# First stage of a fused attention and two-expert kernel: the first chunk's scores ahead of its decays, the gate tables on two queues

## The chip, the cores and the metric

The kernel runs on one core of a Trainium2 chip. The metric is the device time of one execution in microseconds (us), lower is better. [...] The other engines are VectorE (DVE), ScalarE (ACT), GpSimd (POOL) and SyncE (SP), which here only issues DMAs.

## The reference, cut to what matters

```python
for t in range(S):                                  # B, H, S, D = 4, 8, 768, 40
    m_new = maximum(f_gate[t] + m, i_gate[t])       # running maximum of the gates
    f_stab = exp(f_gate[t] + m - m_new); i_stab = exp(i_gate[t] - m_new); m = m_new
    C = f_stab * C + i_stab * outer(v[t], k[t])     # state of each head, 40 x 40
    n = f_stab * n + i_stab * k[t]
    y[t] = sigmoid(o_gate[t]) * (C @ q[t]) / maximum(abs(n @ q[t]), 1)
x = moe(y)      # 3072 tokens of 320: each goes to one of 8 experts, 320 -> 1024 -> 320, times its gates
return moe2(x)  # (sigmoid(x @ w_gate) * (x @ w_val)) @ w_out, 320 -> 1536 -> 320
```

## The kernel before, in words

The recurrence over 768 positions is computed in chunks of T = 128, six to a sequence, 24 in all (`NTILE`). Within a chunk the output is (scores times decays) times values, with the decay of two positions as the exponential of a difference of running gate sums; between chunks a state of 40 x 41 per head is carried. The gates are worked out for all 32 rows (sequence and head) at once, in two halves of 384 positions: `gates(x)` (L477) is a chain on VectorE of a scan, five elementwise operations and a second scan, with two roundings on ScalarE (L493, L496) and a subtraction on GpSimd (L485). `store(x)` (L508) writes four results to two DRAM tables, `L_d` and `a_d`; `decay(u)` (L412) reads them back, spread over partitions, into the operands `at` and `rt` for three chunks at a time. `pattern_at` and `pattern_rt` (L468, L473) fill the fixed rows of these operands. `factors(x)` and `exps(x)` (L516, L522) make the per-token factors; `to_end(x)` (L527) transposes them on TensorE into `tm` and makes the gate totals `gt` by one more product, from `own_g`.

For a chunk, `dec` (L636) makes the exponents of the decays in PSUM (for chunk 0 directly from the gates, with small products, L642 to L647; for the others from `at` and `rt`, L651), `exp` (L653) the decays, `sc` (L657) the scores of q and k, `pf` (L662) their product, each in two groups g of four heads. `out_` (L675) multiplies by the values, `inter` (L685) adds the carried state, `kw` (L670, GpSimd) and `state` (L700) make the chunk's own state, `Cm`, `C`, `cb` carry it on. `den`, `th` (tanh of the output gate, ScalarE, L739), `th1` (adds 1, GpSimd, L742), `sod` (GpSimd) and `x` finish the attention; `xh`, `xla`, `xl`, `tr`, `log` make the split row and its routing logits; `route` ranks tokens, and `scatter` (L848, GpSimd) writes each 128 rows to their experts' places in DRAM. The first expert's job reads the first 16 tiles of rows back with a transposing DMA (L337).

Every engine runs its instructions in the order in which the program issues them, and every DMA is issued from one engine's queue in that order. `begin()` (L547) and `first()` (L588) issue the stage up to the end of chunk 0. After that `step(n)` (L927) walks the list `ORDER` (L40), where `name:lag` issues that part for chunk n - lag, and `r:k` takes up to k pieces from the generator `step.route`. In step 1 that generator is `rest` (L620): the remaining pieces of the second half's gates, its store, factors, pattern, exponentials, `decay(1)` and chunk 3's loads, in this order. `step` issues the loads of chunk n + 2 at its start, on SP, for n > 1 (L936), so those of chunk 4 stand ahead of `decay(1)` and of chunk 3's. `warm(n)` (L613) issues products of zeros whose results nobody reads; `WARM` = 22 of them open the program.

After the attention come the experts' jobs and the second block (L1112 on), where three quarters of the time lie and nothing changes.

## Time and profile before

| what | us |
|---|---|
| median of 3 runs | 727.23 |
| lowest, highest | 726.78, 731.73 |
| the profiled execution | 726.39 |
| its span | 724.3 |
| TensorE busy in the span | 698.8 |

The span reaches from the first to the last instruction that the profile records; the execution's time is 2.1 us longer. Starts in the timelines count from the span's start. A stretch is read from the windows, which give each engine's busy time in it and the granted clock; a wait is read from the timeline, whose bracket behind an instruction gives the idle time of its engine ahead of it and what ended that.

### The profile page before, as it was taken

To read this page: it belongs to the slowest core of one execution; us is meant where nothing else is said; L and a number is where in the kernel's file an instruction comes from. 1 tells how busy PE (TensorE), PEld (TensorE's weight loads), DVE (VectorE), ACT (ScalarE), POOL (GpSimd) and SP (SyncE) were. 2 spreads that over 40 slices of the span, in tenths; PEclk is the share of its full clock that TensorE was granted. 3 is DMA by queue.
4 is the path that set the end of the run, shared out by engine and by line. 5 is a ranking of instruction groups with operands and counts; after the bars stand their busy time and mean duration, and the time that the engine had idled before them with its cause. 6 is when DMAs were issued, how large, how long until landed. Compare 5 with 4: busy or idle time off the path is not lost. (4 is left out here: it accounts for less than half of the span.)

```text
span 724.3 us, 15451 instructions
## 1 busy us (share of the span) xinstructions
PE 698.8 (96%) x6048; PEld 495.2 (68%) x6048; DVE 396.7 (55%) x912; ACT 328.1 (45%) x782; POOL 144.8 (20%) x172
## 2 busy tenths in 40 slices
PE   8899999869999999999989999999999999999998
PEld 5799998857666775667656676666666666666665
DVE  6767678627788879898877810322403223032230
ACT  5477787625575666654545511322313223132231
POOL 5456788842211121221100000000000000000000
PEclk8799999988999999999999999999999999999999
DMA  6466667543999998873525013001020020000000
GB/s 192 130 183 178 199 185 215 174 143 87 273 297 292 266 274 234 253 232 108 139 59 138 21 35 76 0 19 37 1 55 1 10 47 1 28 1 10 19 0 28
DMA packets 67131, 84.02 MB, mean 116 GB/s; under 512 B 41401, under 2 KB 48970, under 8 KB 67058
## 3 DMA queue, kind: packets, MB, share of 16 engines
q1 hardware_dynamic: 63824, 73.35, 36.1%
q0 software_dynamic: 2640, 9.33, 3.6%
q8 instruction: 48, 0.79, 0.5%
q10 hardware_dynamic: 594, 0.35, 0.2%
q14 instruction: 25, 0.20, 0.1%
HBM read 57.53 MB, written 17.16 MB: 103 GB/s over the span
## 5 line engine op out<-in xcount | busy, mean ns | idle before, releaser
L125 PE MATMUL pa<-xT,wgv 128*128 128x384 f16 x1536 | 250.9, 326 | 2.8 <-DVE hh L1166 2.1
L125 PEld LDWEIGHTS <-wgv 128*128 128x128 f16 x1536 | 150.2, 98 | 102.2 <-issue 3.4
L1161 DVE SCALAR_TENSOR_TENSOR gt<-pa,sg 128x384 f32<-128x384 f32 x96 | 53.5, 557 | 224.2 <-PE pa L125 193.3
L1179 PE MATMUL pb<-wo,hh 128*128 128x320 f16 x864 | 118.5, 299 | 0.0
L1160 ACT ACTIVATE sg<-pa 128x384 f32<-128x384 f32 x96 | 47.0, 490 | 143.7 <-PE pa L125 143.7
L1179 PEld LDWEIGHTS <-hh 128*128 128x128 f16 x864 | 84.5, 98 | 33.2
L358 PE MATMUL pb<-w,hh 128*128 128x320 f16 (+4 forms) x624 | 86.6, 299 | 0.0
L125 PE MATMUL pa<-xT,w 128*128 128x384 f16 (+5 forms) x576 | 80.9, 301 | 1.6 <-DVE hh L348 1.6
L358 PEld LDWEIGHTS <-hh 128*128 128x128 f16 (+4 forms) x624 | 62.8, 101 | 22.3 <-DVE hh L348 0.5
L125 PEld LDWEIGHTS <-w 128*128 128x128 f16 x640 | 55.7, 98 | 32.6 <-issue 2.6
L112 DVE SCALAR_TENSOR_TENSOR w<-ws,w 128x512 f16<-128x512 f32 (+1 forms) x92 | 56.1, 642 | 4.7 <-ACT w L111 3.9
L111 ACT ACTIVATE w<-ws 128x512 f16<-128x512 f32 (+1 forms) x92 | 50.3, 592 | 13.1 <-DMA ws<-in_w 11.7
L1181 ACT ACTIVATE ob<-pb 128x320 f32<-128x320 f32 x24 | 10.5, 437 | 100.5 <-PE pb L1179 100.5
L660 PE MATMUL ps<-qk 128*128 128x128 f32 x384 | 53.9, 287 | 0.0
L1166 DVE TENSOR_TENSOR hh<-gt,hh 128x384 f16<-128x384 f32 x96 | 52.7, 549 | 0.7
L369 POOL DMA_INDIRECT y_d<-yr,own x24 | 28.0, 1167 | 125.0 <-ACT w L111 19.5
L1165 ACT ACTIVATE hh<-gt 128x384 f16<-128x384 f32 x96 | 49.4, 515 | 5.9 <-DVE gt L1161 5.9
L660 PEld LDWEIGHTS ps<-qk 128*128 128x128 f32 x384 | 49.9, 203 | 1.0 <-issue 0.2
L665 DVE TENSOR_TENSOR pf<-ps,w 128x512 f32<-128x512 f32 x48 | 33.0, 686 | 21.7 <-ACT w L655 11.4
L347 ACT ACTIVATE hh<-pa 128x384 f16<-128x384 f32 (+6 forms) x80 | 33.4, 431 | 13.8 <-PE pa L125 13.1
L348 DVE SCALAR_TENSOR_TENSOR hh<-pa,hh 128x384 f16<-128x384 f32 (+6 forms) x80 | 36.3, 480 | 3.9 <-ACT hh L347 3.6
L655 ACT ACTIVATE w<-pw 128x512 f32<-128x512 f32 x48 | 28.3, 592 | 1.4 <-PE pw L651 0.5
(185 smaller groups left out, 716.5 us busy)
## 6 DMA issues: line engine op xcount, KB each, us to landing
ws<-in_w SPq DMA_DIRECT2D x24, 512.0 KB
vk<-in_vk SPq DMA_DIRECT2D x24, 324.0 KB
qk<-in_qk SPq DMA_DIRECT2D x48, 160.0 KB
ws<-in_w SPq DMA_DIRECT2D x15, 480.0 KB
ws<-in_wg SPq DMA_DIRECT2D x9, 512.0 KB
ws<-in_wv SPq DMA_DIRECT2D x9, 512.0 KB
ws<-in_wo SPq DMA_DIRECT2D x8, 480.0 KB
out<-ob SPq DMA_DIRECT2D x24, 160.0 KB
```

The source lines that it names most:

```text
L111: A.activation(hi, src, AF.Copy, scale=scale)
L112: low = lambda: V.scalar_tensor_tensor(lo, src, scale, hi, ALU.mult, ALU.subtract)
L125: PE.matmul(ps, r if swap else l, l if swap else r, start=n == 0, stop=n == len(steps) - 1)
L347: A.activation(self.hh[:, 0, f], ph, AF.Relu)
L348: V.scalar_tensor_tensor(self.hh[:, 1, f], ph, 0.0, self.hh[:, 0, f], ALU.max, ALU.subtract)
L358: PE.matmul(py, self.hh[:, x, k, sl], w2[:, y, k, :], start=k == 0 and x + y == 0, stop=k == K1 - 1 and x == 1)
L660: PE.matmul(m.ps[g][:, p, :], m.k2[:, g, p], m.q2[:, p], start=True, stop=True)
L1160: A.activation(sg, pgv[0], AF.Sigmoid, scale=1.0 / (SY * SWG))
L1161: V.scalar_tensor_tensor(gt, pgv[1], SGT / (SY * SWV), sg, ALU.mult, ALU.mult)
L1165: A.activation(self.gh[:, 0, f, :], box[0], AF.Copy)
L1166: V.tensor_sub(self.gh[:, 1, f, :], box[0], self.gh[:, 0, f, :])
L1179: PE.matmul(po, self.gh[:, x, k, sl], wo[:, y, k * DM:(k + 1) * DM], start=k == 0 and x + y == 0, stop=k == K2 - 1 and x == 1)
```

## The change

The scores of chunk 0 are issued ahead of its decays, those of chunk 1 at the end of the first stage (`sc0`, `sc1` leave step 1). `store` and the reads of `a_d` take a queue; for the first half it is ScalarE's, while `L_d` stays on SP. Chunk 1's loads move ahead of the first half's store, `c32` ahead of chunk 0's values, chunk 2's loads behind the zeroing of their buffer, which moves from GpSimd to ScalarE. Output gates and constants are issued by GpSimd, later than before. Factors and pattern of the first half change places; the second half's pattern is copied by ScalarE. The second half's gates begin in step 1 and not in `first()`. `to_end` hands back its last product as `spread`, which is issued later. Three warm-up products at the end of `first()` go, two come at the start. `th1` moves from GpSimd to VectorE.

```diff
         def decay(u):
+            rows(u, SP_)
+            blocks(u)
+
+        def rows(u, queue):
+            c0 = u % 2 * HC
+            tk = slice(c0 * T, (c0 + HC) * T)
+            src = a_d[:, :, u // 2 * 2:u // 2 * 2 + 2, tk].rearrange("n h g s -> (n h) g s")
+            for i in range(2):
+                queue.dma_start(out=at[0:8, i, :, tk], in_=src)
+
+        def blocks(u):
             b, c0 = u // 2, u % 2 * HC
             c1 = c0 + HC
-            tk = slice(c0 * T, c1 * T)
-            src = a_d[:, :, 2 * b:2 * b + 2, tk].rearrange("n h g s -> (n h) g s")
-            for i in range(2):
-                SP_.dma_start(out=at[0:8, i, :, tk], in_=src)
             for g in range(2):
...
                 copy(at[:, k].rearrange("p g (c t) -> p g c t", t=T)[:, :, cs],
                      cat[:, k:k + 1, :].unsqueeze(1).to_broadcast([KM, 2, len(range(NC)[cs]), T]))
-        def pattern_rt(cs):
-            V.tensor_copy(rt[:, :, cs].rearrange("p g c h t -> p g c (h t)"),
-                          crt.rearrange("p h t -> p (h t)").unsqueeze(1).unsqueeze(1).to_broadcast([KM, 2, len(range(NC)[cs]), NP * T]))
+        def pattern_rt(cs, copy):
+            copy(rt[:, :, cs].rearrange("p g c h t -> p g c (h t)"),
+                 crt.rearrange("p h t -> p (h t)").unsqueeze(1).unsqueeze(1).to_broadcast([KM, 2, len(range(NC)[cs]), NP * T]))
         def gates(x):
...
             SP_.dma_start(out=L_d.rearrange("n g x -> (n g x)").rearrange("(p x y) -> p x y", p=128, y=n),
                           in_=zr.unsqueeze(1).to_broadcast([128, 2, n]))
-        def store(x):
+        def store(x, queue):
             h = half(x)
...
                 SP_.dma_start(out=blocks, in_=c3(aL[:, 2 + n, h]))
-                SP_.dma_start(out=a_d[n].rearrange("h g s -> g h s")[:, :, h], in_=aL[:, n, h])
+                queue.dma_start(out=a_d[n].rearrange("h g s -> g h s")[:, :, h], in_=aL[:, n, h])
         def factors(x, eng):
...
                             c3(fg[:, half(x)])[:, :, T - 1].unsqueeze(1).to_broadcast([R, B * NP, HC]), ALU.mult)
-            pl = psC.tile([128, B * NP * HC], F32, name="pl", tag="c")
-            PE.matmul(pl, side, own.rearrange("r b c -> r (b c)"), start=True, stop=True)
-            V.tensor_copy(gt[:, x].rearrange("q b p c -> q (b p c)"), pl)
+
+            def spread():
+                pl = psC.tile([128, B * NP * HC], F32, name="pl", tag="c")
+                PE.matmul(pl, side, own.rearrange("r b c -> r (b c)"), start=True, stop=True)
+                V.tensor_copy(gt[:, x].rearrange("q b p c -> q (b p c)"), pl)
+
+            return spread
         blank = small.tile([1, 8], F32, name="blank", bufs=1)
         DIRECT = 1
...
             load_qk(chunks[0])
+            SP_.dma_start(out=c32, in_=a["c32"])
             load_v(chunks[0])
-            SP_.dma_start(out=c32, in_=a["c32"])
             zeros = kws[1].rearrange("p h x -> p (h x)")
             copy(qks[1].rearrange("q x p t -> q x (p t)"), zeros.unsqueeze(1).to_broadcast([128, 3, NP * T]))
+            load_qk(chunks[1])
+            load_v(chunks[1])
             pattern_at(H0, copy)
...
                 pass
-
-            G.tensor_copy(blank, L[0:1, S // 2 - 8:S // 2])
-            output_gates(0, G)
-            G.memset(qks[2], 0.0)
-            output_gates(1, G)
-            pattern_rt(H0)
+            store(0, A)
             factors(0, V)
-            store(0)
-            load_qk(chunks[1])
-            load_v(chunks[1])
-            decay(0)
             exps(0)
+            pattern_rt(H0, V.tensor_copy)
+            blocks(0)
+
+        def first():
+
+            m = chunks[0]
+            copy = lambda o, i: A.activation(o, i, AF.Copy)
+            zeros = kws[1].rearrange("p h x -> p (h x)")
+            for g in range(2):
+                sc(m, g)
+            warm(2)
+            for g in range(2):
+                dec(m, g)
+            for g in range(2):
+                exp(m, g)
+                pf(m, g)
+            spread = to_end(0)
+            rows(0, A)
+            copy(qks[2].rearrange("q x p t -> q x (p t)"), zeros.unsqueeze(1).to_broadcast([128, 3, NP * T]))
+            for t in Cbs:
+                copy(t.rearrange("q p j d -> q (p j d)"), zeros[:, :NP * 2 * DV])
             load_qk(chunks[2])
             load_v(chunks[2])
-
-        def first():
-
-            m = chunks[0]
-            dec(m, 0)
-            dec(m, 1)
-            later = gates(1)
-            for _ in range(2):
-                next(later)
-            for g in range(2):
-                exp(m, g)
-                sc(m, g)
-                pf(m, g)
-            warm(2)
-            for t in Cbs:
-                A.activation(t.rearrange("q p j d -> q (p j d)"), kws[1].rearrange("p h x -> p (h x)")[:, :NP * 2 * DV], AF.Copy)
-            to_end(0)
             kw(m)
+            for t, name in ((c16, "c16"), (tok, "tok")):
+                G.dma_start(out=t, in_=a[name])
+            output_gates(0, G)
             for g in range(2):
                 out_(m, g)
+            for g in range(2):
+                sc(chunks[1], g)
+            spread()
             state(m)
-            warm(3)
-            for t, name in ((c16, "c16"), (tok, "tok"), (wgl_s, "wgl"), (ctab, "ctab")):
-                A.dma_start(out=t, in_=a[name])
-            step.route = rest(later)
+            pattern_rt(H1, copy)
+            step.route = rest()
         def warm(n):
...
             for _ in range(n):
                 PE.matmul(pz, z[:, 0:128], z[:, 0:512], start=True, stop=True)
-        def rest(later):
-
-            yield from later
-            yield
-            store(1)
+        def rest():
+
+            yield from gates(1)
+            yield
+            store(1, SP_)
+            factors(1, G)
             yield True
-            factors(1, G)
-            yield
-            pattern_rt(H1)
-            yield
             exps(1)
...
             A.activation(gate(m.t)[:, 0], gate(m.t)[:, 0], AF.Tanh, scale=0.5)
         def th1(m):
-            G.tensor_scalar_add(gate(m.t)[:, 0], gate(m.t)[:, 0], 1.0)
+            V.tensor_scalar_add(gate(m.t)[:, 0], gate(m.t)[:, 0], 1.0)
         def x(m):
...
                         out_of(1)
-                elif name in ("tr", "ev", "log", "lg") and n >= NTILE or name[:3] == "out" and n == 1:
+                elif name in ("tr", "ev", "log", "lg") and n >= NTILE or name in SOONER and n == 1:
                     pass
...
                         assert not pending or pending[-1][0] < EARLY
                         blank_rows(first_end(), SLOTS[0] - HEAD)
+                    if n == 1 and name == "kw":
+                        for t, dram_ in ((wgl_s, "wgl"), (ctab, "ctab")):
+                            G.dma_start(out=t, in_=a[dram_])
+                        output_gates(1, G)
                     if n == 2 and name == "pf0":
-                        to_end(1)
+                        step.spread = to_end(1)
+                    if n == 2 and name == "state":
+                        step.spread()
                     if n >= (NTILE - 1 if name != "sod" else 20) and name in ("kw", "sod", "xla"):
...
                     G.memset(blank, 0.0)
                 scatter()
-        UPS, WARM = 6, 22
+        UPS, WARM = 6, 24
+        SOONER = ("sc0", "sc1", "out0", "out1")
         LOADS = {21: [0], 22: [1], 23: [2], 24: [3, 4], 25: [5]}
```

## Rows read from the trace of the kernel before

**Rows 1.** Page, part 1 (busy time of an engine) and part 5 (groups).

```profile
PE 698.8 (96%) x6048; PEld 495.2 (68%) x6048; DVE 396.7 (55%) x912; ACT 328.1 (45%) x782; POOL 144.8 (20%) x172
...
L665 DVE TENSOR_TENSOR pf<-ps,w 128x512 f32<-128x512 f32 x48 | 33.0, 686 | 21.7 <-ACT w L655 11.4
...
L655 ACT ACTIVATE w<-pw 128x512 f32<-128x512 f32 x48 | 28.3, 592 | 1.4 <-PE pw L651 0.5
```

**Rows 2.** Windows: stretch, length, engines' busy us, PEclk, DMA share, GB/s.

```profile
10.80:17.60 6.80, 6.80 (x40) 5.44 (x37) 4.56 (x7) 2.62 (x6) 2.44 (x3) 0.50 0.83 239
21.00:24.40 3.40, 3.40 (x14) 2.49 (x15) 2.62 (x5) 1.49 (x4) 0.96 (x1) 0.51 0.64 187
31.20:38.10 6.90, 6.83 (x81) 6.63 (x82) 3.07 (x10) 3.87 (x13) 3.74 (x7) 0.51 0.68 197
```

**Rows 3.** Windows of three steps of attention, columns as in rows 2.

```profile
42.00:46.90 4.90, 4.90 (x100) 4.75 (x98) 3.00 (x8) 4.18 (x13) 2.75 (x5) 1.00 0.50 138
126.97:132.51 5.54, 5.07 (x101) 4.78 (x98) 4.23 (x12) 4.18 (x13) 5.07 (x7) 1.00 0.93 294
132.51:138.17 5.66, 5.07 (x99) 4.77 (x98) 3.57 (x9) 4.18 (x13) 5.19 (x7) 1.00 0.53 204
```

**Rows 4.** Timeline of PE: start us, duration us, line, operation, idle before.

```profile
1.30 6.23 PE L618 MATMUL pz<-kw 128*128 128x512 f16 x22 [1.30 <-POOL blank L553]
...
11.00 0.61 PE L642 MATMUL pw<-ws 97*128 97x256 f16 x2
...
13.35 3.78 PE L660 MATMUL ps<-qk 128*128 128x128 f32 x16
...
19.38 1.13 PE L683 MATMUL po<-vk,pf 128*64 128x41 f32 x32
...
26.95 1.05 PE L660 MATMUL ps<-qk 128*128 128x128 f32 x8
...
31.27 0.62 PE L540 MATMUL pl<-own_g,c 32*128 32x48 f32 x2 [1.66 <-DVE own_g L537]
...
36.56 1.80 PE L660 MATMUL ps<-qk 128*128 128x128 f32 x8
```

**Rows 5.** Timeline of DVE, both halves' gates, the pattern copies.

```profile
3.78 1.01 DVE L482 TENSOR_TENSOR_SCAN ws<-w,ws 32x384 f32<-32x384 f32 x1 [2.94 <-DMA w<-in_fi]
...
9.45 0.55 DVE L500 TENSOR_TENSOR w<-w,w 32x384 f16<-32x384 f32 x1
9.92 1.98 DVE L474 COPY rt<-ws 97x3072 f16<-97x3072 f16 x1
...
12.76 1.00 DVE L482 TENSOR_TENSOR_SCAN ws<-w,ws 32x384 f32<-32x384 f32 x1
...
25.60 0.54 DVE L500 TENSOR_TENSOR w<-w,w 32x384 f16<-32x384 f32 x1
```

**Rows 6.** Timeline of SP's issues, the loads of chunks 0 and 3.

```profile
3.44 1.38 SPq L428 DMA_DIRECT2D qk<-in_qk  x2
...
31.10 1.32 SPq L428 DMA_DIRECT2D qk<-in_qk  x2
32.52 0.43 SPq L432 DMA_DIRECT2D vk<-in_vk  x1
```

**Rows 7.** Timeline of POOL, the wait for chunk 3's values.

```profile
37.15 0.72 POOL L673 TENSOR_TENSOR kw<-vk,tm 128x320 f32<-128x320 f32 x1 [0.35 <-DMA vk<-in_vk]
```

**Rows 8.** Timeline of ACT: pattern copies, scaled states of step 1.

```profile
4.70 3.02 ACT L549 ACTIVATE at<-ws 97x768 f16<-97x768 f16 x4
...
25.41 0.97 ACT L710 ACTIVATE Cm<-Cst,gt 128x41 f32<-128x41 f32 x4
```

**Rows 9.** Timeline of POOL in the step of chunk 22.

```profile
137.96 1.02 POOL L743 TENSOR_SCALAR hh<-hh 128x320 f32<-128x320 f32 x1
```

**Rows 10.** Timeline of SP: the transposing read of the routed rows.

```profile
142.71 1.49 SPq L337 DMA_TRANSPOSE hh<-xs_d  x1
```

**Rows 11.** Line L732: duration min/median/max in ns, first and last start.

```profile
L732 DVE TENSOR_SCALAR den<-den x24: 149/392/677, 28.6 to 148.9; 128x8 f32<-128x8 f32 x24
```

## The prediction, made before the result was known

> **What bounds the kernel now.** I read the page first. TensorE is busy for 698.8 us of a span of 724.3 [rows 1], so time can be won only where TensorE waits or runs at its lower clock. [...]
>
> Then the timelines. TensorE runs 22 warm-up products until 7.53, both groups' decays until 13.35 and the 16 score products at the lower clock from 13.35 [rows 4]. In step 2 it waits 1.66 us for own_g [rows 4], which VectorE makes late, behind its second pattern copy. VectorE runs the first half's gates from 3.78 to 10.00 and starts the second half's scan at 12.76, long before it is needed; their last operation ends at 26.14 [rows 5]. What hangs on that is a queue: after the store of this operation's result SP issues chunk 4's loads, the tables of the second half, then chunk 3's, whose issue ends at 32.42 (q and k) and 32.95 (values) [rows 6]. GpSimd waits for those values until 37.15 [rows 7], 4.2 us after their issue, and chunk 3's scores start at 36.56 [rows 4]. So both TensorE's work and this queue end at about the same time at the entry of step 3.
>
> **The change part by part.**
>
> *Scores first.* 24 warm-ups end at about 1.30 + 24 x 0.28 = 8.1 [rows 4]. Chunk 0's q and k, issued until 4.82 [rows 6], land at the latest 4.2 later by the rate of rows 7, at 9.0, and at 8.1 at the earliest that matters; I take 8.6. The 16 scores at the full clock are two times 1.05 [rows 4], to 10.7. Two warm-ups, 0.5. A group's decays take 2.35 at the lower clock (11.00 to 13.35 [rows 4]), 1.2 at the full one: both end at 13.6. Before, scores and decays together ended near 17.1 (13.35 + 3.78). So 3.5 us are won here.
>
> *What follows on VectorE.* Factors and pattern copy change places; with 0.9 and 1.98 [rows 5] both end at 12.9, when the first group's exponential (decays until 12.4, and 0.59 [rows 1]) is just done, so this swap costs nothing. Exponential 0.59 and product 0.69 [rows 1] after the last decay: 14.9. The second half of chunk 0's output products, 0.57 of 1.13 [rows 4]: 15.5. Now chunk 1's 16 scores come ahead of the gate totals: 2.1 at the full clock, 3.78 at the lower [rows 4]. Which level is granted there no row shows: in the run before the decays ran without a pause from 11.00 at the lower level and it stayed, until the scores had run for some 4 us [rows 2, 4]. I take the middle, 18.4, and 0.6 for the totals [rows 4] and their copy: 19.0, with 18.1 and 19.8 as the ends.
>
> *The second half's gates.* This is the part that costs. They no longer begin at 12.76, but behind that copy, at 19.0, since VectorE works in order. The first half's took 6.2 us from scan to last operation (3.78 to 10.00 [rows 5]), without anything between. In step 1 stand between them the first state (0.3, an estimate below the 0.69 of a product), the first product, 0.69 [rows 1], and on ScalarE an exponential, 0.59 [rows 1], and four scaled states, 0.97 [rows 8], ahead of the rounding that the last operation needs; of these 1.56 I count 1.3. Sum: 19.0 + 6.2 + 0.3 + 0.7 + 1.3 = 27.5, against 26.14: **1.4 us later**, although TensorE is ahead at this point (ends: 26.6 and 28.3, so 0.5 to 2.2 later).
>
> *Tables on two queues, loads moved.* ScalarE now issues the first half's two stores and two reads of a_d, SP those of L_d, without chunk 1's loads and the output gates between store and read. By the steps above chunk 1's decays stand behind chunk 0's state, at about 19.5, and the tables have 6 us from their pattern at 12.9 to land, more than the 4.2 of rows 7: hidden; were it 7.6, the loss would be 1. On ScalarE the four issues take up to 0.7 each (two on SP took 1.32 [rows 6]); the stores lie before the first exponential, where ScalarE waits for the decays. The reads wait there for their stores to land, and behind them stand the zeroings, the pattern and step 1's first exponential; by 4.2 after a store issued at 10.7 that wait ends at 14.9, at most 1 after the engine comes to it, and the slack below covers 0.5. For the second half all stores stay on SP in the old order, so the 1.4 us reach chunk 3's loads in full: issue ends at 33.8 and not at 32.42, landing by at most 37.9. GpSimd's five issues (constants and output gates) fall where it waits for VectorE's gates; the scaled keys of chunks 0 and 1 stand ahead of them: nothing, or up to 1 if the gates' subtraction had to wait. The three warm-ups that go at the end of the first stage, 0.28 each [rows 4], stood where TensorE now waits anyway: nothing.
>
> *Pattern by ScalarE.* ScalarE took 3.02 for 4 x 768 elements [rows 8], so about 3 us for one copy of the same 3072, ahead of the first exponential of step 1: 14.2 + 2.2 for the zeroings of 2192 elements (an estimate at that rate) + 3.0 = 19.4, when the decays come too: hidden, and 1 late if the reads above wait. VectorE loses 2 us of step 2 (the same size as the first copy [rows 5]) and the totals no longer stop TensorE for 1.66 [rows 4]. What is late next is chunk 3's q and k: TensorE would be through with step 2 by 36.56 - 1.66 = 34.9 and waits for them. So of this gain nothing arrives in step 3.
>
> *Step 3.* The scores start up to 1.4 later than 36.56; if before they waited for TensorE and not for the load, 0.4: I take **1.1**. TensorE stands still for some 2 us ahead of them, in a stretch that before ended at the full clock from 38.10 [rows 2]. Another stretch at the lower clock, 3.4 as the one from 21.00 [rows 2], costs half, 1.7; none costs 0. I take **1.0**. Head: +2.1. The lower end is -2: gates ending as before, step 3 starting 0.4 sooner and at the full clock, where before 36.56 to 38.10 ran at the lower (0.8), and 0.8 for a load that lands sooner. The upper end is +4.9: 2.2, 1.7 and the 1 of the reads.
>
> *The tanh's add on VectorE.* On GpSimd it takes 1.02 [rows 9] in all 24 steps. In the steady loop GpSimd waits anyway (2.75 busy of 4.90 [rows 3]). In the two steps from 126.97 it does not: 5.07 of 5.54 and 5.19 of 5.66 [rows 3], TensorE idle for 0.47 and 0.59, since each step then carries two scatters. With 1.02 less TensorE bounds them again: -1.06. The scatters lead to the transposing read at 142.71 [rows 10], on which the experts wait, so it arrives. VectorE gets the operation: nearest by size is the product pf, 0.69 for 512 elements [rows 1], so 0.43 for 320; nearest by kind den with 8 elements, 0.15 to 0.68 [rows 11]. I take 0.35, between them; hidden in PE-bound steps, and lost once, where a step is full of routing on VectorE: +0.2 to +0.7 there. **Tail: -0.8**, ends -1.4 and +0.5.
>
> [...] The den row varies by a factor of 4.5 at one size [rows 11]. [...]
>
> **Sum.** The profiled execution took 726.39 (span 724.3 and 2.1 around it), the median of the runs is 727.23, 0.84 more. 2.1 - 0.8 = +1.3: 727.7 on the profiled execution's scale, **728.5 us** on the median's. A measurement of this kernel can tell about 1%, 7.3 us, from no change.
>
> **The rivals.**
>
> *The gates are not late (faster).* If the full clock holds through chunk 1's scores, the scan starts at 18.1 or sooner, the last operation ends at 26 and chunk 3's loads are issued as before. TensorE then enters step 3 waiting less, and runs it at the full clock. For: the 1.7 us pause behind the warm-ups, after which the clock fell, is gone. Against: the decays alone never raised it. Price: head -2, tail -1: 724.2. Were the loads also sooner, 722.
>
> *The clock stays down (slower).* The mechanism is the idle of TensorE in step 3. If it waits longest for chunk 3's q and k, the lower clock holds from 38 to 45, as long as the one from 31.20 to 38.10 [rows 2]: half of 6.9, 3.4, with the load's 2.2 that is +5.6 and a tail of 0: 732.8. It decides from the point where the last gate operation ends after 28.3. For: 31.20 to 38.10 was such a stretch, behind a wait of 1.66. Against: step 3 itself has 16 scores, behind which the clock rose each time.
>
> *It moves nothing.* The scores were never the bound of the head, and what ends last at step 3's entry is the queue on SP, whose order stays. If the gates end at 26.1 and the clock is as before, only the tail counts: 726.4.
>
> **How the numbers follow.** Forecast 0.5, gates in time 0.2, clock down 0.15, nothing moved 0.15. The range takes in the first rival's 724 and the second's 733, and cuts off what lies beyond: 723 to 732.5. Only a case outside all four is faster than 720 (0.04); past 734.5 lies the end of the second rival with a tail of +0.5, and more (0.08).
>
> **What would show it.** Right: the second scan starts at 18 to 20, its last operation ends at 26.6 to 28.3, the scores of chunk 0 end by 11; chunk 3's scores start at 37 or later, behind an idle of TensorE; the wait for own_g is gone; the two steps near 130 take 4.9 to 5.1. Wrong: steady steps (PE busy throughout, 4.90 long) from before 37; a scatter step still over 5.5; VectorE's added operation above 0.7.

## The result, and the profile after

| | before | after |
|---|---|---|
| median, lowest, highest of 20 runs each (us) | 726.71, 722.45, 731.73 | 731.82, 728.90, 737.60 |
| ratio after to before, 95% interval | | 1.0085 [1.0062, 1.0108] |
| the profiled execution, its span (us) | 726.39, 724.3 | 729.70, 727.9 |

The change made the kernel slower by 5.1 us. That is less than the 1% which the text above takes as no change, but with twenty runs each it is clear of the noise, and it is four times the +1.3 that was forecast: 731.82 lies at the upper end of the range and not near 728.5. The spans of the profiled pair differ by 3.6 us.

TensorE (PE in the rows) is busy for as long as before, 698.9 us against 698.8, so on balance those 3.6 us are waits; GpSimd's busy time falls from 144.8 to 116.1 us [rows 1]. The page of the changed kernel, part 1:

```profile
PE 698.9 (96%) x6047; PEld 493.4 (68%) x6047; DVE 398.7 (55%) x935; ACT 331.9 (46%) x784; POOL 116.1 (16%) x150
```

The head first. Timeline of TensorE in the changed kernel (L669 scores, L538 transposes of the second half's factors, L660 decays):

```profile
9.25 1.95 PE L669 MATMUL ps<-qk 128*128 128x128 f32 x16
...
16.17 2.05 PE L669 MATMUL ps<-qk 128*128 128x128 f32 x16
...
28.62 0.36 PE L538 MATMUL pg<-c,w 32*128 32x32 f32 x3 [1.45 <-ACT w L531]
29.49 0.37 PE L538 MATMUL pg<-c,w 32*128 32x32 f32 x3 [0.51 <-ACT w L532]
...
37.47 2.05 PE L669 MATMUL ps<-qk 128*128 128x128 f32 x8 [1.60 <-DMA qk<-in_qk]
39.31 0.63 PE L660 MATMUL pw<-rt,at 97*128 97x256 f16 x2
39.73 1.68 PE L669 MATMUL ps<-qk 128*128 128x128 f32 x8
...
43.92 0.39 PE L660 MATMUL pw<-rt,at 97*128 97x256 f16 x2
```

In the two profiles of this pair the granted clock is 1.00, the upper, or 0.50, the lower, and nothing between. Chunk 0's 16 scores take 1.95 at the upper clock (1.00 over 9.25 to 11.20) instead of 3.78 [rows 4] at the lower (0.50 over 13.35 to 17.13) and end at 11.2, 5.9 us sooner. Chunk 1's decays start at 19.10 and not at 22.08, so TensorE is 3 us ahead there. In steps 2 and 3 it loses that again: from 23.3 to 37.5 it waits 6.4 us in eight places, where before the timeline shows one wait in these steps, the 1.66 for own_g. The longest are the 1.45 and 0.51 for the exponentials of the second half's factors, and the 1.60 for chunk 3's q and k. Chunk 3's scores start 0.91 later than in [rows 4], and chunk 4's decays, where the steady loop begins, at 43.92 against 41.98: **+1.94**.

Why these come late: the second half's gates. Timelines of VectorE (L489 the scan, L491 the add, L507 the last gate operation) and SP:

```profile
18.73 1.00 DVE L489 TENSOR_TENSOR_SCAN ws<-w,ws 32x384 f32<-32x384 f32 x1
...
19.88 1.21 DVE L491 TENSOR_TENSOR w<-w,ws 32x384 f32<-32x384 f32 x1
...
26.55 0.55 DVE L507 TENSOR_TENSOR w<-w,w 32x384 f16<-32x384 f32 x1 [0.60 <-ACT w L503]
```

```profile
27.80 0.65 SPq L521 DMA_DIRECT2D a_d<-w  x1
...
32.52 1.32 SPq L435 DMA_DIRECT2D qk<-in_qk  x2
33.94 0.43 SPq L439 DMA_DIRECT2D vk<-in_vk  x1
```

The scan stands at 18.73 instead of 12.76 [rows 5], since it is issued behind the copy of the gate totals (L550, 18.61), for which VectorE sat idle for 2.65 us; the last operation ends at 27.10 instead of 26.14, its store goes out at 27.80, and chunk 3's loads are issued 1.42 later than in [rows 6]. The values land a little later still: chunk 3's scaled keys wait until 38.71, against 37.15 [rows 7]. The pattern on ScalarE (L595) is nearly hidden: the exponential behind it starts at 19.76, when the first of chunk 1's decays (from 19.10 on) have been there for some 0.3 us. Timelines of GpSimd and ScalarE:

```profile
38.71 0.72 POOL L682 TENSOR_TENSOR kw<-vk,tm 128x320 f32<-128x320 f32 x1 [2.56 <-DMA vk<-in_vk]
```

```profile
17.11 2.75 ACT L595 ACTIVATE rt<-ws 97x3072 f16<-97x3072 f16 x1
```

Windows of the changed kernel (columns as in rows 2): the stretch at the lower clock, a steady step, and the three steps that answer to the last two of [rows 3] and the one ahead of them:

```profile
30.80:41.00 10.20, 7.54 (x62) 6.71 (x59) 4.00 (x16) 4.56 (x14) 2.73 (x6) 0.50 0.74 213
43.92:48.84 4.92, 4.92 (x101) 4.78 (x98) 3.06 (x9) 4.18 (x13) 1.93 (x3) 1.00 0.51 137
122.89:128.35 5.46, 5.11 (x102) 4.89 (x99) 5.18 (x25) 4.30 (x13) 3.86 (x5) 1.00 0.64 185
128.35:133.50 5.15, 5.15 (x100) 4.96 (x98) 3.16 (x10) 4.27 (x13) 4.15 (x5) 1.00 0.87 281
133.50:138.74 5.24, 5.17 (x101) 4.93 (x99) 3.26 (x10) 4.26 (x14) 4.16 (x5) 1.00 0.72 272
```

Step 3 runs almost wholly at the lower clock, until 41.0 and not until 38.1 [rows 2]. The steps with two scatters are bound by TensorE again, 5.15 and 5.24 against 5.54 and 5.66 [rows 3]; the step ahead of them took 6.09 before (120.88 to 126.97) and takes 5.46. The changed kernel is 2.01 late where these three steps begin and 0.57 where they end, and the first expert's transposing read is issued only 0.32 later than in [rows 10]: of the head's 1.94 the loop gave back 1.62, nearly all of it here, where GpSimd no longer makes the add.

Behind that the profiled pair drifts apart again. The second transposing read (of the rows scattered last) is 2.09 late. The difference is 1.80 where TensorE goes on behind its wait near 380 us (381.66 against 379.86); there the changed kernel has 3.4 us at the lower clock, which the other lacks in this profile, and from 395 us to the end the difference stands at 3.5: TensorE had no wait in that stretch, and it cost half its length (3.5 less 1.80).

### The profile page after: what moved, and what is told of

It reads as the page before. It is cut to its first block, busy times and chain, and to the rows that moved or that the text cites. A ratio compares the mean times of both kernels' runs of the same rounds, so it can differ in the third digit from the quotient of the medians.

```text
span 727.9 us, 15447 instructions
## 1 busy us (share of the span) xinstructions
PE 698.9 (96%) x6047; PEld 493.4 (68%) x6047; DVE 398.7 (55%) x935; ACT 331.9 (46%) x784; POOL 116.1 (16%) x150
## 5 line engine op out<-in xcount | busy, mean ns | idle before, releaser
L1197 ACT ACTIVATE ob<-pb 128x320 f32<-128x320 f32 x24 | 10.5, 437 | 100.5 <-PE pb L1195 100.5
L669 PE MATMUL ps<-qk 128*128 128x128 f32 x384 | 52.2, 281 | 2.5 <-DMA qk<-in_qk 1.6
L669 PEld LDWEIGHTS ps<-qk 128*128 128x128 f32 x384 | 48.1, 197 | 4.4 <-issue 2.0
L369 POOL DMA_INDIRECT y_d<-yr,own x24 | 28.3, 1180 | 127.2 <-DVE w L112 31.7
```

What stands on the lines that cost most here:

```text
L669: PE.matmul(m.ps[g][:, p, :], m.k2[:, g, p], m.q2[:, p], start=True, stop=True)
```

## The experiments

Eighteen runs: eight edited kernels, one of them twice, and the two kernels above again. Where a kernel was timed, its ratio stands against runs of the kernel before on the same chip; three chips were used.

**The gates begun early again.**

```diff
+            later = gates(1)
             for g in range(2):
+                next(later)
                 exp(m, g)
                 pf(m, g)
             spread = to_end(0)
+            for _ in range(2):
+                next(later)
...
-            step.route = rest()
+            step.route = rest(later)
```

> The changed kernel with the first four pieces of the second half's gates issued in the first stage again (scan, add, two subtractions, scaling), two of them ahead of the products pf of chunk 0 and two behind the copies of the factors, where VectorE waits 1.47, 0.63 and 2.65 us. Theory: the second scan starts at 12 to 13, the last gate operation ends at 23 to 25 instead of 27.10, chunk 3's loads are issued 2 to 3 us sooner, chunk 4's decays start at 41 to 42.5 instead of 43.92, ratio 1.004 to 1.006. Rival (what ends step 2 is not the gates but TensorE's own work at the lower clock): chunk 4's decays at 43 or later, ratio 1.0075 or more.

Measured 0.9954 [0.9925, 0.9982], 723.5 us: the way that was expected, and far more than expected. Timelines of VectorE (gates) and TensorE:

```profile
12.10 1.00 DVE L489 TENSOR_TENSOR_SCAN ws<-w,ws 32x384 f32<-32x384 f32 x1
...
22.93 0.55 DVE L507 TENSOR_TENSOR w<-w,w 32x384 f16<-32x384 f32 x1
```

```profile
33.49 0.39 PE L664 MATMUL pw<-rt,at 97*128 97x256 f16 x2
33.72 1.05 PE L673 MATMUL ps<-qk 128*128 128x128 f32 x8
...
38.10 0.48 PE L780 MATMUL pt<-c,xsb 128*128 128x128 f16 x5
```

The last gate operation starts at 22.93. From 18 us on TensorE waits in two places only (1.54 and 0.30), step 3 begins at 33.49 with scores at the upper clock, and chunk 4's decays stand at 38.42, 5.5 us ahead of the changed kernel and 3.6 ahead of the kernel before. The lower clock held from 14.8 to 28.4 here, 13.6 us against the 10.2 from 30.8 in the changed kernel, but it was over when step 3 began. With the other parts of the change in place, this one turns its loss into a gain.

**The gates late alone**, in the kernel before: its two `next(later)` go, and `rest` begins with `gates(1)`.

> The kernel before with this one part of the change: the second half's gates do not begin in the first stage, but in step 1. Theory (the late start of these gates is the loss): the second scan starts at 21 to 23 instead of 12.76, the last gate operation ends at 29 to 32 instead of 26.14, chunk 3's scores start at 39 to 42 behind a wait of TensorE, chunk 4's decays at 44.5 to 47.5 instead of 41.98, ratio 1.007 to 1.013. Rival (the loss of the change comes from its other parts, the moved loads and the two queues): ratio 1.003 or less.

Measured 1.004 [1.0012, 1.0067], 732.5 us against 728.5. Timelines of VectorE and TensorE:

```profile
16.38 1.00 DVE L482 TENSOR_TENSOR_SCAN ws<-w,ws 32x384 f32<-32x384 f32 x1
...
27.34 0.55 DVE L500 TENSOR_TENSOR w<-w,w 32x384 f16<-32x384 f32 x1 [0.60 <-ACT w L496]
```

```profile
30.98 0.37 PE L531 MATMUL pg<-c,w 32*128 32x32 f32 x3 [2.49 <-ACT w L524]
...
38.46 1.05 PE L657 MATMUL ps<-qk 128*128 128x128 f32 x8
```

Only 1.7 us later than in [rows 5], less than I had said, because VectorE came to the scan sooner. It is enough for a slower kernel: 0.4%, about half of the 0.85% above, and nearly all of the 0.48% that the change itself cost in the same comparison. The wait that it makes is not the one expected: chunk 3's q and k are there in time, TensorE waits 2.49 us for the exponential of the factors, and chunk 4's decays are at 43.16. (One profile; the kernel before has them between 41.29 and 43.63 in three.)

**Chunk 3's loads early** (right behind chunk 2's; gone from behind `decay(1)`), which takes away the wait on SP's queue and leaves the gates late.

> The changed kernel with chunk 3's loads issued right behind chunk 2's, not behind the second half's tables. Theory (the late gates cost through SP's queue alone): the wait of 1.60 us for q and k ahead of chunk 3's scores is gone, they start at 35.6 to 36.2 instead of 37.47, chunk 4's decays at 42.0 to 42.7 instead of 43.92, ratio 1.0055 to 1.0065. Rival one (the exponentials and tables of the second half are late as well and become the next wait): chunk 4's decays at 43.4 or later, ratio 1.008. Rival two (the head is not where the measured loss comes from): chunk 4's decays start sooner as said, and the ratio stays at 1.008 to 1.009.

Measured 1.0093 [1.0056, 1.0129]. Timeline of TensorE: chunk 3's scores, and the first expert's products.

```profile
36.53 1.91 PE L669 MATMUL ps<-qk 128*128 128x128 f32 x8
...
42.39 0.45 PE L776 MATMUL pt<-c,xsb 128*128 128x128 f16 x5
42.68 0.39 PE L660 MATMUL pw<-rt,at 97*128 97x256 f16 x2
...
184.82 9.55 PE L125 MATMUL pa<-hh,w 128*128 128x256 f16 x64 [6.01 <-DMA hh<-xs_d]
```

The wait for q and k is gone and chunk 4's decays are 1.24 sooner than in the first profile of the change, as the theory has it; yet the ratio is no better. In this profile the gain is lost at 184.82 to a new wait of 6.01 us for the transposing read. That read comes behind the last scatter. Timelines of GpSimd and VectorE there:

```profile
172.01 7.71 POOL L859 DMA_INDIRECT xs_d<-xsb,dest  x1 [0.21 <-issue]
```

```profile
172.11 4.82 DVE L112 SCALAR_TENSOR_TENSOR w<-ws,w 128x512 f16<-128x512 f32 x8
176.86 2.01 DVE L112 SCALAR_TENSOR_TENSOR w<-qk,w 128x480 f16<-128x480 f32 x4
```

GpSimd's issue of that scatter took 7.71 us, about as long as VectorE's weight splitting beside it; in the kernel before and the changed one it took 0.97. So this run says that the queue's share of the head is 1.24 us against the first profile of the change (2.2 against the mean of eight, below), and says nothing of the total.

**Both**: gates and loads early.

> The changed kernel with the second half's gates begun in the first stage and chunk 3's loads behind chunk 2's. With the gates in time (0.9954 in that run, chunk 4's decays at 38.42, steps of 4.93 from 33.49 on) the theory says that SP's queue is no longer what TensorE waits for: chunk 4's decays at 38.0 to 38.6, ratio 0.994 to 0.997, no different from the gates alone. Rival (loads are still the next wait): chunk 4's decays at 37.5 or sooner, ratio 0.993 or less.

Measured 1.002 [1.0002, 1.0038]. The head is the earliest of all, chunk 4's decays at 37.32, so the loads were worth another 1.1 us (the rival's 37.5), though a wait for q and k of 0.73 at 43.36 took most of that back. The same scatter took 7.71 us again, and TensorE waited 5.55 us for the read behind it: that is about what it lost against the gates alone (1.002 against 0.9954, 0.7%, though on another chip).

**The add.** Back on GpSimd in the changed kernel (`V.tensor_scalar_add` to `G.tensor_scalar_add` in `th1`), and on VectorE in the kernel before:

> The changed kernel with one part undone: the tanh's add back on GpSimd. Theory (the change loses 1.9 us in the head through the late gates of the second half, and wins 1.1 to 1.4 in the two steps that carry two scatters): those two steps take 5.5 to 5.7 us again instead of 5.15 and 5.24, the transposing read is issued 1.1 to 1.4 later, ratio to the kernel before 1.010 to 1.0105, against 1.0085 of the full change. Rival (the add on VectorE costs more than it gives, further on or at VectorE): the ratio falls to 1.006 or less. If the head's state at step 4 is as in the changed kernel, chunk 4's decays start at 43.9.

> The kernel before with this one part of the change: the tanh's add on VectorE. Theory: steady steps stay at 4.90 us or less, chunk 4's decays start at 42.0 as before, the two steps with two scatters take 5.1 to 5.25 instead of 5.54 and 5.66, the transposing read is issued at 141.3 to 141.6 instead of 142.71, ratio 0.998 to 0.9985. Rival (the add costs on VectorE): ratio 1.001 or more, with VectorE named as the releaser of idle time of TensorE.

Measured 1.0046 [1.0022, 1.0069] for the change without it and 0.9991 [0.9963, 1.002] for it alone. The steps moved as said: 5.70 and 5.67 without it, 5.16 and 5.23 with it, and alone it brought the transposing read from 142.71 to 140.72. The total did not follow: without the add on VectorE the changed kernel is no slower, where 1.010 was expected (the rival had 1.006 or less). Where the 2 us went in the second pair can be followed in its two profiles: the first expert's products (L888), the read ahead of them, and the routing product behind them (L806). Timelines of SP and TensorE with the add on VectorE, and of TensorE in the kernel before:

```profile
140.72 1.49 SPq L337 DMA_TRANSPOSE hh<-xs_d  x1
```

```profile
146.64 8.00 PE L888 MATMUL pa<-hh,ws 128*128 128x256 f32 x24 [3.82 <-issue]
154.48 0.18 PE L806 MATMUL pr<-oh,c 128*128 128x40 f16 x1
```

```profile
147.82 6.87 PE L888 MATMUL pa<-hh,ws 128*128 128x256 f32 x24 [3.66 <-issue]
154.52 0.18 PE L806 MATMUL pr<-oh,c 128*128 128x40 f16 x1
```

And the windows of the lower clock, first with the add on VectorE, then in the kernel before:

```profile
145.00:151.80 6.80, 5.16 (x12) 4.21 (x13) 4.13 (x16) 1.90 (x6) 2.14 (x3) 0.50 0.69 227
```

```profile
147.30:150.70 3.40, 2.88 (x7) 2.38 (x8) 2.06 (x8) 0.92 (x4) 2.41 (x3) 0.51 0.64 258
```

From the issue of the read to the products it takes 5.92 and not 5.11, and the products 8.00 and not 6.87: the lower clock lies over 5.16 us of them and not 2.88 (PE busy in the two windows), and half of that difference is 1.14, the 1.13 by which they are longer. The routing product comes at the same time, 154.5. How much of this is chance two profiles can't tell: from the read to the routing product it took 11.81 and 13.76 here, and in the unaltered kernels 11.1 to 12.8 (three profiles of the kernel before) and 11.2 to 14.1 (eight of the changed one).

With the gates early, and the add on GpSimd:

> The changed kernel with the second half's gates begun in the first stage and the tanh's add back on GpSimd. The add on VectorE made the transposing read 2.0 us earlier in the kernel before and 1.4 to 2.2 in the changed one, but the runs show no gain in the end (0.9991 where it was put alone, 1.0046 where it was taken back out). Theory (the gain in the loop is given back while the attention drains, so the gates alone carry the result): ratio 0.993 to 0.998, not different from 0.9954, two scatter steps of 5.5 to 5.7 us, chunk 4's decays at 38 to 39. Rival (the add's gain counts once the head is in time): ratio 0.998 or more.

Measured 0.9941 [0.9914, 0.9968], 723.8 against 727.1 us: no worse than with the add on VectorE. In none of the three pairs did the move show a gain beyond the intervals; each interval is some 2 us wide to either side, so a gain of 0.8 is not shut out either.

**Waits of TensorE filled** with products that nobody reads (`busy(n)` issues n of them), gates left late:

```diff
+                    if (n, name) in FILLS:
+                        busy(FILLS[n, name])
                     parts[name](chunks[n - lag])
+                    if n == 2 and name == "pf0":
+                        busy(6)
...
+        FILLS = {(1, "inter"): 5, (2, "dec1"): 3, (3, "sc0"): 6}
```

> The changed kernel with products that nobody reads put into four waits of TensorE (5 ahead of chunk 1's carried state, 3 ahead of the second decays of step 2, 6 ahead of the transposes of the second half's factors, 6 ahead of chunk 3's scores), the late gates left as they are. Theory (each such wait also costs by a stretch at the lower clock behind it): chunk 3's scores take 1.05 and not 2.05 us a group, chunk 4's decays start at 42 to 43.3 instead of 43.92, mean granted clock 0.979 or more, ratio 1.002 to 1.005. Rival (the waits cost by their length alone): chunk 4's decays at 43.5 or later, ratio 1.008 or more.

Measured 1.0012 [0.9993, 1.0031]; the mean granted clock is 0.983, against 0.976 of the changed kernel in the same comparison. Timeline of TensorE:

```profile
37.13 2.72 PE L636 MATMUL pz<-ws 97*128 97x512 f16 x6 [0.36 <-ACT xTu L786]
39.64 1.92 PE L675 MATMUL ps<-qk 128*128 128x128 f32 x8
```

The head did not go as expected: the filling took 2.72 us where 1.60 were free, 0.45 a product against 0.28 for the warm-ups [rows 4], so by this estimate it ran at the lower clock itself, and chunk 4's decays came at 45.78. The total is the better one all the same, 729.3 us against 732.4: the means of the runs are 3.4 us apart, with 25.2 us at the lower clock against 34.9 (worked out from the granted clocks as below). It fits a loss through the clock, but this profile doesn't show where the clock was won, so it is support and no proof.

**The same kernels again**, to see what a profile of one execution is worth.

> The changed kernel, unaltered, for a second profile and more runs. Over 20 runs its mean granted clock was 0.9757, over 29 runs of the kernel before 0.983: 35.6 us at the lower level against 24.7 (twice the missing share times the span). Theory (most of the measured loss is time at the lower clock, of which the first profile, with a clock of 0.981, shows little): the mean granted clock is 0.974 to 0.977 again, the ratio 1.007 to 1.010, and this profile shows stretches at 0.5 in the head or behind the attention that the first one lacks; chunk 4's decays start at 43.5 to 45.5. Rival (the first profile stands for the kernel): clock 0.98 or more, ratio 1.005 or less.

> The kernel before, unaltered, for a second profile. Theory (the change raises the time at the lower clock; over all runs so far 25.5 us a run in the kernel before, 35.4 in the changed one): 20 to 30 us at 0.5 in this profile, none of it between 180 and 400; chunk 4's decays at 41.5 to 42.5, the transposing read of the first expert issued at 142 to 143.5. Rival (where the lower clock falls is the same chance in both kernels): 30 us or more, with a stretch near 380.

> The changed kernel, unaltered, for a third profile, beside the kernel before on the same chip. Theory: chunk 4's decays at 43.5 to 45.5 (43.92 and 44.86 in the first two), 30 to 42 us at the lower clock, of them 10 to 17 in the head, 10 to 14 between 140 and 175 and 3 to 10 between 180 and 400. Rival (the first two profiles met the stretch near 382 by chance): none between 180 and 400.

> The changed kernel, unaltered, for a profile of a run with more time at the lower clock (over 28 runs 35.4 us, in the four profiles so far 30 to 37). Theory one (the extra lies in the head, where the gates come late): at 33 us or more in all, 20 or more of them before 50 us, chunk 4's decays at 45.5 or later. Theory two (it lies behind the attention, at the waits of TensorE near 147, 165, 200 and 382): 10 to 17 before 50 us and 20 or more behind 140 us. Rival (no more than in the kernel before): 30 or less.

> The kernel before, unaltered, for a third profile (over 77 runs 25 us at the lower clock, in its two profiles 30 and 33). Theory: 20 to 28 us at 0.5, 13 to 17 of them before 50 us and no more than 10 behind 140 us ahead of the last 4 us; chunk 4's decays at 41.5 to 43.7. Rival (the place is the same chance in both kernels): 17 or more behind 140 us.

(The fourth, sixth and seventh profile of the changed kernel had the expectation of the third and the fifth.) The second timing of the changed kernel gave 1.0048 [1.0022, 1.0074], with a mean granted clock of 0.976. Starts in us, the first line of each kernel from the pair above:

| profile | chunk 4's decays | first expert's read | second read | span | clock |
|---|---|---|---|---|---|
| before | 41.98 | 142.71 | 173.88 | 724.3 | 0.981 |
| second | 43.63 | 144.08 | 174.41 | 728.7 | 0.976 |
| third | 41.29 | 141.74 | 171.49 | 725.2 | 0.986 |
| after | 43.92 | 143.03 | 175.97 | 727.9 | 0.981 |
| second | 44.86 | 143.90 | 174.41 | 728.8 | 0.979 |
| third | 44.04 | 143.04 | 176.67 | 731.9 | 0.979 |
| fourth | 45.01 | 143.98 | 176.75 | 728.7 | 0.979 |
| fifth | 44.29 | 143.08 | 171.83 | 724.1 | 0.981 |
| sixth | 45.72 | 144.52 | 175.58 | 726.5 | 0.979 |
| seventh | 45.85 | 144.62 | 172.97 | 724.7 | 0.979 |
| eighth | 44.99 | 143.79 | 174.85 | 726.7 | 0.978 |
| mean after less mean before | +2.5 | +0.9 | +1.6 | +1.3 | |

The head's loss is in every profile of the changed kernel: the earliest of its eight starts is later than the latest of three before. So is what the loop gives back: from chunk 4's decays to the first read it takes 98.8 to 99.1 us in the eight profiles and 100.5 to 100.7 in the three. Behind the read the eleven scatter: the routing product starts 1.8 later on the mean, between 154.3 and 158.6 against 154.5 and 155.2.

The stretch at the lower clock near 382 us is in six of the eight profiles of the changed kernel and in the second of the three before. So it is not the change's alone; whether the change makes it more frequent so few can't tell.

Of the theories on the lower clock none held throughout. The fifth profile has 27.4 us of it in all, as the rival had said; the sixth and seventh have 20.5 before 50 us, as theory one, and chunk 4's decays latest of all; none has the 20 us behind 140 that theory two wanted. The second profile of the kernel before has 34.4 in all and the third 20.9, so one profile of either kernel does not stand for its mean. By place, the eight have on the mean 15.8 us before 50, 11.1 between 140 and 180 and 3.0 between 180 and 400; the three have 14.8, 10.2 and 2.3. The profiles show 1.3 us of a difference that the timings put at 4 to 5; with spans from 724.1 to 731.9 that mean is itself uncertain by some 3 us (an estimate from their scatter).

The timed runs, of which only the mean granted clock is left, say more. With the two levels 0.50 and 1.00, twice the missing share times the span is the time at the lower clock (27.4 us for the first profile of the kernel before, whose stretches at that clock add up to 27.3). It is 34.8 us on the mean of 34 runs of the changed kernel and 25.0 in 93 of the kernel before; with the gates early it was 20 to 24. Among runs of one kernel in one comparison, one with 1 us more of it took 0.31 us longer (a line fitted to these 127 runs). By that line 9.8 us more go with 3.0 us, of the 5.0 between the two means (732.1 and 727.2). The other 2.0 are of the size of the head's loss, but of that only 0.9 is left at the first read, so about 1 us stays open. And the line is a correlation: a run in which something came late would show both more time and more of the lower clock. No experiment moved the clock alone.

**Side by side on one chip**, the last comparison:

> The changed kernel, unaltered, timed again beside the next one. Its ratio came out at 1.0085 and 1.0048 in two comparisons; on the chip of the last profiles three runs took 725.9 to 728.3 against 725.0 and 727.3. Theory (a loss of 2 to 2.5 us in the head, plus time at the lower clock that differs from chip to chip): ratio 1.003 to 1.009, mean granted clock under that of the kernel before. Rival (the loss is of the first chip): 0.998 to 1.002.

> The changed kernel with the second half's gates begun in the first stage, as in the run that gave 0.9954, beside the changed kernel on the same chip. Theory (their late start is what turns the change into a loss): 0.993 to 0.998, and 0.8% to 1.3% under the changed kernel in the same call; the last gate operation ends at 22.5 to 23.5, chunk 4's decays at 38 to 39. Rival (chance of the chip): less than 0.4% under it.

Measured 1.0089 [1.0062, 1.0115] for the change, 728.8 us, and 0.9953 [0.9925, 0.998] with its gates begun early, 721.3: 1.0% under it, with the kernel before at 723.9 between them. In the profiles of the two, chunk 4's decays are at 44.99 and 38.53, 6.5 us apart; so the head can account for most of the 7.5 us between them.

## Why the prediction was wrong, point by point

*Right: the head, its cause and its size.* Scores of chunk 0 end at 11.2 (said: by 11), the second scan starts at 18.73 (19.0), the last gate operation ends at 27.10 (27.5), chunk 3's loads are issued until 33.84 (33.8), its scores start 0.91 late (1.1), and the lower clock in step 3 makes that 1.94 at chunk 4 (1.0 more). The head's sum was +2.1; the first pair has 1.94, the mean of the profiles 2.5. Some of this is luck. The 19.0 was the middle between two clocks for chunk 1's scores; the upper one was granted (16 scores in 2.05), for which the same sum says 18.1, and the scan came at 18.73 because these scores began at 16.17 and not at 15.5. Chunk 0's scores and decays ended at 14.16, 3.0 ahead of before and not 3.5, and the pattern copy, counted with 1.98, took 0.94. That the late gates are the cause is shown from both sides: begun early the change gains 0.5% instead of losing 0.9% (they then also end 2.7 to 3.5 us ahead of the kernel before, 22.66 and 23.48 against 26.14), late alone the kernel before loses 0.4%.

That the head's loss goes through the steady loop unchanged holds for its steps: 4.90 before [rows 3] and 4.92 after, with TensorE busy for all of both, and 1.94 at chunk 4 is 2.01 where the three steps near 130 begin. There the scatters bound the kernel before, and most of the 1.62 came back.

*Incomplete: what is late next.* I let the gates act through SP's queue alone. They act twice: TensorE also waits for the exponentials of the same half (1.45 and 0.51), and where the queue was cleared the head gained 1.24 of its 1.94.

*Wrong in part: the tail of −0.8.* The step is "on which the experts wait, so it arrives". Up to the read the gain was twice that, 1.62, and it is in every profile; the sum had counted two steps, and the one ahead of them won 0.63 as well. From the read to the routing product 0.9 of it is gone on the mean of the profiles, in the pair with the add alone all of it, by a slower read and a longer stretch at the lower clock. Three pairs of kernels show no gain in the time; what was wrong is to carry a gain at the read to the end as it stood, while a total of −0.8 is neither shown nor shut out. The operation itself I had rightly small: 0.35 was taken, 0.29 is its median. The rows of the line of the changed kernel (min, median, max in ns), and of the longest one with GpSimd's beside it:

```profile
L752 DVE TENSOR_SCALAR hh<-hh x24: 275/290/866, 27.3 to 150.5; 128x320 f32<-128x320 f32 x24
```

```profile
27.34 0.87 DVE L752 TENSOR_SCALAR hh<-hh 128x320 f32<-128x320 f32 x1
```

```profile
27.19 0.82 POOL L526 TENSOR_TENSOR w<-w,w 32x384 f32<-32x384 f32 x1 [3.92 <-DVE den L741]
```

The one long case is the one that starts beside a GpSimd operation; it ends at 28.21, 0.20 behind the end of that operation. In the other 23 GpSimd ran no operation beside, and they took 0.33 at most. That GpSimd held it up is not shown: the two fall together once in 24, and no run tests it.

*Wrong: the term for the lower clock.* This is the step that failed by the most. "I take **1.0**" is for step 3; for the rest of the kernel the sum has nothing, and gives no reason. In step 3 it was right, with a stretch of 10.2 and not of 3.4 us: 0.91 became 1.94. Over the whole kernel the timed runs have 9.8 us more at this clock, 34.8 against 25.0, which by the fitted line go with 3.0 us. That is the larger part of the missing 3.8 (+1.3 said, 5.1 measured), as far as a correlation can say. Where most of it falls stays open: the profiled executions have only 2.8 us more of it (30.3 against 27.5), a little at each of the three places.

*The rivals.* The slower one named the lower clock and 732.8, near the result, but that is luck, since its place was wrong: in the first profile the gates ended at 27.1, ahead of its 28.3 (27.0 to 28.2 in all eight), and the lower clock held from 30.8 to 41.0, not from 38 to 45, with +1.94 and not +5.6 behind it. The faster one, gates in time at 724.2, is near what the experiment made of the change, 723.5, with gates that end some 3 us sooner than this rival has them.

## What to carry to other kernels

A chain of small operations on an engine with spare time is worth starting as soon as its inputs are there, in the gaps between other work: here four pieces of it, moved from behind the first stage into VectorE's gaps, turned a loss of 0.9% into a gain of 0.5%, on one chip side by side. When a step is moved late, follow all that hangs on its end, the direct consumer as well as the queue. And a gain at a point ahead of a stage with waits of its own is a forecast for that point only, until the stage's end is timed.

## What was not expected of the hardware

The two kernels with chunk 3's loads early had one indirect DMA whose issue on GpSimd took 7.71 us, beside 12 splitting operations of VectorE (4.82 and 2.01 us) that started 0.1 us behind it. In the kernel with the gates alone early the same pair started as close together, 0.13 us apart, and the issue took 0.98. Timelines of GpSimd and VectorE there:

```profile
167.02 0.98 POOL L863 DMA_INDIRECT xs_d<-xsb,dest  x1 [0.21 <-issue]
```

```profile
167.15 4.82 DVE L112 SCALAR_TENSOR_TENSOR w<-ws,w 128x512 f16<-128x512 f32 x8
```

And the second kernel with the loads early, `a_both`:

```profile
168.21 7.71 POOL L863 DMA_INDIRECT xs_d<-xsb,dest  x1 [0.21 <-issue]
```

```profile
168.30 4.82 DVE L112 SCALAR_TENSOR_TENSOR w<-ws,w 128x512 f16<-128x512 f32 x8
```

In both long cases the issue ended 0.85 us behind the last split. Its 7.71 us are about the 6.76 of the splits and the 0.97 that it takes elsewhere together, as if it had stood while they ran. One number tells the two kinds apart in all twenty profiles. The splits started 0.09 us behind the issue in the two long cases, and 0.12 to 0.19 behind it in the eighteen where the issue took 0.97 or 0.98. Two cases against eighteen sort and do not test: no run moved this start alone.

What ties the issue to the splits no run shows. The order of the starts is not what decided: in the long cases and in the others the issue started first.

The same two engines meet at VectorE's pattern copy of the first half. It took 1.98 in the three profiles of the kernel before [rows 5], beside a GpSimd operation, and 0.94 in the eight of the changed kernel, where GpSimd ran nothing. GpSimd in the kernel before, VectorE in the changed one:

```profile
9.69 1.40 POOL L576 MEMSET qk<- 128x1536 f32 x1
```

```profile
11.10 0.94 DVE L481 COPY rt<-ws 97x3072 f16<-97x3072 f16 x1
```

The time at the lower clock varies by more from run to run than the change moved its mean: 25 to 46 us among the first 20 runs of the changed kernel, worked out from their granted clocks as above.
